# Sliding-window attention and two feed-forward layers: weight tiles without a place of their own use two buffers in turn

## The chip, the core and the metric

The kernel runs on one core of a Trainium2 chip, as one launch. The metric is the device time of one execution in microseconds (us). The engines are PE (TensorE: matmuls; PEld is its weight load), DVE (VectorE), ACT (ScalarE), POOL (GpSimd) and SP (SyncE, which here only issues DMAs). Each engine runs its own instructions in the order in which the program gives them, and waits on semaphores for the others.

## The reference

```python
S, D = 768, 64                      # 2 batches, 8 heads
scores = q @ k.T / sqrt(D) + bias   # 8 global keys, and the 96 newest keys of each query
a = softmax(where(keep, scores, -1e9))
x = (a @ v), heads joined           # 1536 tokens x 512
h = x @ w_in;  g = max(h, 0) + alpha * min(h, 0);      x = g @ w_out      # d_ff = 2048
h = x @ w_in2; g = (a0+a1 h+a2 h^2+a3 h^3) / (1+|b0||h|+|b1|h^2+1e-6);  out = g @ w_out2
```

All of it is float32. The four weight matrices arrive as float64 words, two 32-bit words for each number.

## The kernel before

**Split numbers.** Matmuls run on a rounded float32 format (fp32r). Each operand is kept as a high part and a low part, and a product is three passes: high by high, high by low, low by high.

**Weight jobs.** A weight matrix is cut into chunks `fc` of 128 hidden features, and a job prepares the "in" or the "out" half of one chunk, 128 x 512 numbers. `plan_weights` gives each job the tick at which it starts, and their order makes their number `n`. A job takes three ticks. At its start tick ACT scales the high words into `de` (L324). At the next tick DVE joins the words into `dx` with three instructions (L313, L314, L315); after them the code calls `load_more`, which has SP load the words of a later job (L269). At the third tick (L291 to L307) ACT, or POOL in the first slots, writes the high part `hi` (L301 or L303), and DVE writes the low part `lo` one tick later (L304).

**Where a job's tiles go.** Most jobs write into a slot of weight tiles. While attention runs only four such slots exist. The eight jobs of chunks 8 to 11, numbers 15 and 17 to 23, have no slot (`slot is None`): they write `hi` into `part1` and `lo` into `part2`, and both are sent to DRAM by `spill()` (L209 to L212). `spill()` is called at the third tick of the next job, just before that job's `hi`, and once more ahead of slot 15. SP issues these DMAs in the program's order, so they stand behind the L269 that was issued one tick earlier. The spilled chunks are read back (L217) when attention is over. `part0` to `part3` are tiles of the whole kernel, and `part3` holds the identity for transposes until then.

**Joint slots.** The stretch of the trace that matters here is that of the joint slots s = 8 to 15 (`joint_slot`, L848), in which a step of attention (two pairs of heads, step number u = 10 + s) runs beside one step of the first feed-forward layer. One slot gives each engine, in this order:

- PE: scores of step u (L431), values of step u-2 (L514, L516), `first(s)` = x @ w_in, 12 matmuls (L738), transposes of step u-1 (L490, L492), transposes of new keys or queries (L399, up to slot 10), `second(s-1)` = g @ w_out, 12 matmuls (L804);
- DVE: reciprocal (L465), the bias of step u with its row minimum (L446), `xlo` (L527), the low part of the job before (L304), the join of the next job (L313 to L315), the activation of `first(s)` (L744, L745);
- ACT: four exponentials (L453) with `xhi` among them (L526), copies `pt` (L501), `ghi` (L746), then the job's `hi` (L301) and the scaling of the next job (L324). In slot 8 four copies of results (L820) stand between `ghi` and `hi`;
- POOL: `glo` of the slot before (L747), L464, then the four normalisations of step u-1 (L470).

From slot 16 on attention is gone, its memory becomes the weight slots 4 to 15 (pool `late`, whose tiles each wait for what lay there), and PE runs one matmul after the other.

Of the kernel before, what the change touches and what calls it, by code (L numbers as in the profile page):

```python
# [8 lines left out]
F32 = mybir.dt.float32  # L9
F32R = mybir.dt.float32r  # L10
# [7 lines left out]
P = 128  # L18
# [4 lines left out]
DM = 512  # L23
# [29 lines left out]
def flat(t):  # L53
    return t.rearrange("p c f -> p (c f)")


def words(t):
    return flat(t).bitcast(F32)


class Kernel:
# [222 lines left out]
    def tick(self, on_act, start, spread=False):  # L284
        nc = self.nc
        if self.later:
            self.later.popleft()()
        while self.splits:
            self.splits.popleft()()
        self.join_step(5)  # L290
        if self.pipe and self.pipe[0][0] == "joined":  # L291
            _, n = self.pipe.popleft()
            m, fc, kind, slot = self.plan[n]
            self.spill()
            x = words(self.dx[n % 3])
            if slot is None:
                hi, lo = (t.bitcast(F32R) for t in self.part[1:3])
            else:
                hi, lo = (flat(self.slots[slot][kind, part]) for part in PARTS)
            if on_act:  # L300
                nc.scalar.copy(hi, x)  # L301
            else:
                nc.gpsimd.tensor_scalar(hi, x, 1.0, 1.0, ALU.mult, ALU.mult)  # L303
            self.splits.append(lambda: nc.vector.tensor_sub(lo, x, hi.bitcast(F32)))  # L304
            if m == 0 and fc < KEPT:
                for part, of in zip(PARTS, (hi, lo)):
                    self.unspilled.append((words(self.spilled[fc][kind, part]), of.bitcast(F32)))  # L307
        if self.pipe:
            _, n = self.pipe[0]
            self.pipe[0] = "joined", n  # L310
            low, e, y = self.staged(n)[:, :, :, 0], self.de[n % 2].bitcast(I32), self.dx[n % 3]
            self.join += [
                lambda: nc.vector.tensor_scalar(y, e, 3, None, ALU.logical_shift_left),  # L313
                lambda: nc.vector.scalar_tensor_tensor(y, e, -(2**31), y, ALU.bitwise_and, ALU.bitwise_or),  # L314
                lambda: nc.vector.scalar_tensor_tensor(y, low, 29, y, ALU.logical_shift_right, ALU.bitwise_or),  # L315
                self.load_more,
            ]
        if not spread:
            self.join_step(5)
        if start:  # L320
            n = self.started
            self.started += 1
            self.pipe.append(("scaled", n))
            nc.scalar.mul(self.de[n % 2], self.staged(n)[:, :, :, 1].bitcast(F32), 2.0**-112)  # L324
# [37 lines left out]
    def attention_window(self, pool, moe):  # L362
# [10 lines left out]
        rec = [pool.tile([P, 4], F32, name=f"rec{i}") for i in range(2)]  # L373
        pt = [pool.tile([P, 2, 2, P], F32, name=f"pt{i}") for i in range(4)]
        self.first_saved = [pool.tile([P, DM], F32, name=f"first{d}") for d in range(NC)]

        def load(nm, i):
            if 2 <= i < NBLK:
                self.load_tokens(nm, i, raw[nm][i % 2])
# [258 lines left out]
    def attention_any(self, pool, moe):  # L638
# [16 lines left out]
        pt = pool.tile([P, NB, P], F32, name="a_pt")  # L655
        st = pool.tile([P, 4], F32, name="a_st")
        self.first_saved = [pool.tile([P, DM], F32, name=f"a_first{d}") for d in range(NC)]

        def transposed(dst, scale, nm, i):
            self.load_tokens(nm, i, ra)  # L660
            t = banks[7].rearrange("p (c t) -> p c t", c=NC)
            for c in range(NC):
                nc.tensor.transpose(t[:, c], ra[:, 2 * c : 2 * c + 2].rearrange("p h d -> p (h d)"), ident)
            nc.scalar.mul(dst, t, scale)
# [313 lines left out]
```

## Time and profile before

| | us |
|---|---|
| median of 3 runs | 677.8 |
| lowest and highest | 676.52, 678.18 |
| profiled execution | 678.08 |
| its span, first to last instruction | 676.2 |

| engine | busy us | share of the span |
|---|---|---|
| PE | 631.6 | 93% |
| DVE | 541.6 | 80% |
| ACT | 374.7 | 55% |
| POOL | 195.2 | 29% |

The profile is one execution with every instruction's start and length. Besides busy times it gives what each idle time of an engine ended on, and the chain of waits: from the last instruction back to what released it, and so on. Times below are from the span's start. 1.9 us of the profiled execution lie outside its span. The granted clock (PEclk) is the share of TensorE's full clock that it was allowed, 1.00 for 2.4 GHz.

### The profile page before, as it was taken

The page shows a single profiled execution, that of the slowest core. Times are in us where ns is not written, and L with a number is a line of the kernel's source. Part 1 is how long each engine was busy: PE and PEld are TensorE (multiplying, and loading weights), DVE is VectorE, ACT ScalarE, POOL GpSimd, SP SyncE. Part 2 cuts the span into 40 slices and gives each one's busy share as a digit, 9 for nine tenths or more (in the row PEclk, how much of TensorE's full clock was granted, in tenths as well). Part 3 has the DMA queues.
Part 4 walks back from the last instruction along what each step waited for, and adds up shares of the span by engine and source line. Part 5 has one row for each costly group of instructions (what it writes and reads, how often), then busy time and mean ns, then how long its engine had stood idle before and what let it go on. Part 6 is the DMA issues. An engine that isn't in the chain of part 4 may idle for free.

```text
span 676.2 us, 9567 instructions
## 1 busy us (share of the span) xinstructions
PE 631.6 (93%) x3250; PEld 510.2 (75%) x3250; DVE 541.6 (80%) x982; ACT 374.7 (55%) x782; POOL 195.2 (29%) x278
## 2 busy tenths in 40 slices
PE   7767998998988999999999998999999999999994
PEld 6656766776866888888888876888878888888782
DVE  3687789984654998876879999999999877786984
ACT  2775565665552432333324367777777766766662
POOL 4554334333232322222222212222222222222221
PEclk9897999998999999999999999999999999999997
DMA  8969488876667882331342231121110000300302
GB/s 164 198 165 271 136 249 251 258 221 222 186 225 235 291 317 89 99 121 31 126 155 63 70 117 31 32 95 39 55 62 1 1 1 1 124 1 0 126 0 69
DMA packets 84860, 82.83 MB, mean 123 GB/s; under 512 B 45312, under 2 KB 61952, under 8 KB 84800
## 3 DMA queue, kind: packets, MB, share of 16 engines
q1 hardware_dynamic: 84800, 82.11, 40.5%
q8 instruction: 28, 0.46, 0.3%
q14 instruction: 32, 0.26, 0.1%
HBM read 60.21 MB, written 19.92 MB: 119 GB/s over the span
## 4 chain that ended last, share of the span: by engine, by line
PE 59%; DVE 23%; ACT 6%; DMA 4%; issue 3%; POOL 3%; SPq 0%; DVEq 0%; ACTq 0%; POOLq 0%
PE bank L804 29%; PE bank L738 28%; DVE dx L314 3%; DVE dx L315 3%; DVE dx L313 3%; ACT prob L453 2%; DMA dwouthi_f<-part 2%; DVE prob L446 1%; DVE act L745 1%; DVE act L744 1%; DMA dwinhi_f<-part 1%; DVE xlo L527 1%; DVE klo L407 1%; DVE act L782 1%; POOL glo L747 1%
## 5 line engine op out<-in xcount | busy, mean ns | idle before, releaser
L747 POOL TENSOR_TENSOR glo<-act,ghi 128x512 fp32r<-128x512 f32 x48 | 65.6, 1367 | 225.6 <-ACT ghi L746 202.6
L789 POOL TENSOR_TENSOR glo<-act,ghi 128x512 fp32r<-128x512 f32 (+1 forms) x49 | 65.7, 1340 | 202.1 <-ACT ghi L785 187.2
L746 ACT CAST ghi<-act 128x512 fp32r<-128x512 f32 x48 | 29.8, 621 | 107.6 <-DVE act L745 99.7
L738 PE MATMUL bank<-xhi,winhi_f 128*128 128x512 f32 x256 | 68.4, 389 | 0.0
L738 PE MATMUL bank<-xhi,winlo_f 128*128 128x512 f32 x256 | 68.4, 389 | 0.0
L738 PE MATMUL bank<-xlo,winhi_f 128*128 128x512 f32 x256 | 68.4, 389 | 0.0
L453 ACT ACTIVATE prob<-prob,stat 128x232 f32<-128x232 f32 (+1 forms) x96 | 44.6, 466 | 38.8 <-DVE stat L446 38.7
L738 PEld LDWEIGHTS bank<-xhi,winhi_f 128*128 128x128 f32 x256 | 48.0, 188 | 10.0
L738 PEld LDWEIGHTS bank<-xlo,winhi_f 128*128 128x128 f32 x256 | 48.0, 188 | 10.0
L738 PEld LDWEIGHTS bank<-xhi,winlo_f 128*128 128x128 f32 x256 | 48.0, 188 | 10.0
L315 DVE SCALAR_TENSOR_TENSOR dx<-stage,dx 128x512 int32<-128x512 int32 x64 | 53.5, 836 | 2.2
L314 DVE SCALAR_TENSOR_TENSOR dx<-de,dx 128x512 int32<-128x512 int32 x64 | 51.8, 809 | 2.2
L756 ACT ACTIVATE stage<-bank 128x512 f32<-128x512 f32 (+1 forms) x49 | 28.8, 588 | 37.5 <-PE bank L738 37.4
L765 DVE SCALAR_TENSOR_TENSOR stage<-stage,abs_b 128x512 f32<-128x512 f32 (+1 forms) x49 | 36.2, 739 | 16.3 <-ACT stage L757 16.3
L470 POOL TENSOR_SCALAR prob<-prob,rec 128x232 f32<-128x232 f32 (+1 forms) x96 | 43.0, 464 | 21.7 <-DVE rec L465 14.3
L785 ACT CAST ghi<-act 128x512 fp32r<-128x512 f32 (+1 forms) x49 | 30.1, 614 | 26.5 <-DVE act L782 26.4
L324 ACT ACTIVATE de<-stage 128x512 f32<-128x512 f32 x64 | 42.4, 667 | 2.3 <-DMA stage<-in_moe_w_out_dram 2.3
L804 PE MATMUL bank<-wouthi_f,ghi 128*128 128x512 f32 x144 | 41.3, 392 | 0.6 <-ACT ghi L785 0.6
L744 DVE TENSOR_SCALAR act<-bank,al 128x512 f32<-128x512 f32 x48 | 35.8, 745 | 7.4 <-PE bank L738 7.2
L804 PE MATMUL bank<-wouthi_f,glo 128*128 128x512 f32 x144 | 41.2, 391 | 0.1
L804 PE MATMUL bank<-woutlo_f,ghi 128*128 128x512 f32 x144 | 41.0, 389 | 0.0
L313 DVE TENSOR_SCALAR dx<-de 128x512 int32<-128x512 int32 x64 | 38.0, 594 | 3.5 <-ACT de L324 3.5
(206 smaller groups left out, 1483.5 us busy)
## 6 DMA issues: line engine op xcount, KB each, us to landing
stage<-in_moe_w_in_dram SPq DMA_DIRECT2D x32, 512.0 KB, 4.1
stage<-in_moe_w_out_dram SPq DMA_DIRECT2D x32, 512.0 KB, 4.0
part<-saved_f SPq DMA_DIRECT2D x16, 256.0 KB, 4.3
va<-in_v_dram SPq DMA_DIRECT2D x13, 256.0 KB, 5.0
saved_f<-part SPq DMA_DIRECT2D x12, 256.0 KB, 3.7
out_dram<-part SPq DMA_DIRECT2D x11, 256.0 KB, 2.1
rawk<-in_k_dram SPq DMA_DIRECT2D x10, 256.0 KB, 4.7
rawq<-in_q_dram SPq DMA_DIRECT2D x10, 256.0 KB, 4.6
```

The lines of the kernel that those rows point to most:

```text
L313: lambda: nc.vector.tensor_scalar(y, e, 3, None, ALU.logical_shift_left),
L314: lambda: nc.vector.scalar_tensor_tensor(y, e, -(2**31), y, ALU.bitwise_and, ALU.bitwise_or),
L315: lambda: nc.vector.scalar_tensor_tensor(y, low, 29, y, ALU.logical_shift_right, ALU.bitwise_or),
L324: nc.scalar.mul(self.de[n % 2], self.staged(n)[:, :, :, 1].bitcast(F32), 2.0**-112)
L453: nc.scalar.activation(p[:, j - e, :w], p[:, j - e, :w], AF.Exp, bias=st[:, j : j + 1], scale=-1.0, accum_out=st[:, 4 + j : 5 + j],)
L470: nc.gpsimd.tensor_scalar(p[:, j, :w], p[:, j, :w], r[:, e + j : e + j + 1], 1.0, ALU.mult, ALU.mult)
L738: nc.tensor.matmul(bk, w["in", a][:, c, :], x[:, c, :], start=e == 0, stop=e == len(seq) - 1)
L744: nc.vector.tensor_scalar(t, h, 0.0, self.al[:, fc : fc + 1], ALU.min, ALU.mult)
L747: nc.gpsimd.tensor_tensor(lo, t, hi.bitcast(F32), ALU.subtract)
L765: nc.vector.scalar_tensor_tensor(w, w, self.ab[:, 0:1], ab, ALU.add, ALU.mult)
L789: nc.gpsimd.tensor_tensor(lo, u, hi.bitcast(F32), ALU.subtract)
L804: nc.tensor.matmul(y[d], lhs, rhs, start=begin and e == 0, stop=last and e == 2)
```

## The change

A pair of tiles `spare0`, `spare1` (128 x 512 float32 each) is added to attention's pool, behind `first_saved`. A job without a slot writes to `part1` and `part2` when its number is even and to the new pair when it is odd. The same pair is added to the general attention, which this input does not take.

```diff
             if slot is None:
-                hi, lo = (t.bitcast(F32R) for t in self.part[1:3])
+                hi, lo = (t.bitcast(F32R) for t in (self.part[1:3], self.spare)[n % 2])
             else:
                 hi, lo = (flat(self.slots[slot][kind, part]) for part in PARTS)
...
         self.first_saved = [pool.tile([P, DM], F32, name=f"first{d}") for d in range(NC)]
+        self.spare = [pool.tile([P, DM], F32, name=f"spare{d}") for d in range(2)]
...
         self.first_saved = [pool.tile([P, DM], F32, name=f"a_first{d}") for d in range(NC)]
+        self.spare = [pool.tile([P, DM], F32, name=f"a_spare{d}") for d in range(2)]
```

By their numbers jobs 15, 17, 19, 21 and 23 go to the new pair, and 18, 20 and 22 stay in `part1`, `part2`.

No instruction moves on any engine; what changes is which tile some of them touch and which semaphores they wait for. On ACT, from the end of slot 8 (the last L820 copy) to the `hi` of slot 9, with the semaphores in brackets (DMAHW are those of SP's DMAs), the order before is:

```order
L820 COPY first3_272<-bank7_89 128x512 [waits PE_49]
L301 CAST part1_76<-dx0_96 128x512 [waits DMAHW2_49,Activation_49]
L324 ACTIVATE de1_95<-stage3_93 128x512 [waits DMAHW0_49]
L453 ACTIVATE prob2_256,stat1_261<-prob2_256,stat1_261 128x232 [waits DVE_49,Pool_49]
L453 ACTIVATE prob2_256,stat1_261<-prob2_256,stat1_261 128x232 [waits DVE_49]
L526 CAST xhi2_107<-bank2_84 128x2x128 [waits PE_49]
L453 ACTIVATE prob3_257,stat1_261<-prob3_257,stat1_261 128x232 [waits DVE_49] x2
L501 COPY pt0_265<-bank0_82 128x512 [waits PE_49]
L501 COPY pt1_266<-bank1_83 128x512 [waits PE_49]
L406 CAST khi_248<-bank2_84 128x4x128 [waits DVE_49,PE_49]
L746 CAST ghi1_102<-act1_100 128x512 [waits DVE_49,Pool_49]
L301 CAST part1_76<-dx1_97 128x512 [waits DMAHW5_49,Activation_49]
```

The same rows of the changed kernel:

```order
L822 COPY first3_272<-bank7_89 128x512 [waits PE_49]
L301 CAST part1_76<-dx0_96 128x512
L324 ACTIVATE de1_95<-stage3_93 128x512 [waits DMAHW0_49,Activation_49]
L454 ACTIVATE prob2_256,stat1_261<-prob2_256,stat1_261 128x232 [waits DVE_49,Pool_49]
L454 ACTIVATE prob2_256,stat1_261<-prob2_256,stat1_261 128x232 [waits DVE_49]
L527 CAST xhi2_107<-bank2_84 128x2x128 [waits PE_49]
L454 ACTIVATE prob3_257,stat1_261<-prob3_257,stat1_261 128x232 [waits DVE_49] x2
L502 COPY pt0_265<-bank0_82 128x512 [waits PE_49,Activation_49]
L502 COPY pt1_266<-bank1_83 128x512 [waits PE_49,Activation_49]
L407 CAST khi_248<-bank2_84 128x4x128 [waits DVE_49,PE_49]
L748 CAST ghi1_102<-act1_100 128x512 [waits DVE_49,Pool_49]
L301 CAST spare0_273<-dx1_97 128x512 [waits DMAHW2_49,Activation_49]
```

The `hi` of job 18 (second row) waits for no DMA any more, and that of job 19 (last row) waits for DMAHW2, the DMA that job 18 waited for before, in place of DMAHW5, which is one job later. L324 and the two `pt` copies now also wait for an earlier instruction of ACT itself.

On DVE, after attention (`winlo14` and `woutlo14` being low parts in weight slot 14 of the pool `late`), before:

```order
L304 TENSOR_TENSOR winlo14_f_2359<-dx1_97,winhi14_f_2358 128x512 [waits DMAHW1_49,Activation_49]
L313 TENSOR_SCALAR dx2_98<-de1_95 128x512 [waits Activation_49]
L314 SCALAR_TENSOR_TENSOR dx2_98<-de1_95,dx2_98 128x512 [waits DVE_49]
L315 SCALAR_TENSOR_TENSOR dx2_98<-stage1_91,dx2_98 128x512 [waits DMAHW1_49,DVE_49]
L744 TENSOR_SCALAR act1_100<-bank0_82,al_66 128x512 [waits PE_49,Pool_49]
L745 SCALAR_TENSOR_TENSOR act1_100<-bank0_82,act1_100 128x512 [waits DVE_49]
L304 TENSOR_TENSOR woutlo14_f_2361<-dx2_98,wouthi14_f_2360 128x512 [waits Activation_49]
```

and in the changed kernel:

```order
L304 TENSOR_TENSOR winlo14_f_2361<-dx1_97,winhi14_f_2360 128x512 [waits DMAHW6_49,DMAHW1_49,Activation_49]
L313 TENSOR_SCALAR dx2_98<-de1_95 128x512 [waits Activation_49]
L314 SCALAR_TENSOR_TENSOR dx2_98<-de1_95,dx2_98 128x512 [waits DVE_49]
L315 SCALAR_TENSOR_TENSOR dx2_98<-stage1_91,dx2_98 128x512 [waits DMAHW1_49,DVE_49]
L746 TENSOR_SCALAR act1_100<-bank0_82,al_66 128x512 [waits PE_49,Pool_49]
L747 SCALAR_TENSOR_TENSOR act1_100<-bank0_82,act1_100 128x512 [waits DVE_49]
L304 TENSOR_TENSOR woutlo14_f_2363<-dx2_98,wouthi14_f_2362 128x512 [waits DMAHW7_49,Activation_49]
```

The two low parts gained a wait each, for DMAHW6 and DMAHW7: the last spill, job 23's, reads the new pair, and `winlo14` and `woutlo14` now lie where that pair lay.

## Rows read from the trace of the kernel before

**Rows 1.** Busy time by stretch: joint slots 8 to 14 by PE's starts, slot 16 on.

```profile
core 0: us, PE busy (x) PEld busy (x) DVE busy (x) ACT busy (x) POOL busy (x), PEclk, DMA share, GB/s
141.72:150.78 9.06, 8.97 (x67) 7.30 (x66) 7.01 (x19) 5.45 (x15) 3.52 (x6) 1.00 0.64 180
150.78:164.75 13.97, 10.71 (x66) 8.43 (x66) 6.81 (x19) 7.96 (x20) 3.66 (x7) 0.88 0.52 173
164.75:173.65 8.90, 8.90 (x66) 7.30 (x65) 5.33 (x16) 4.79 (x14) 2.83 (x6) 1.00 0.77 253
173.65:182.11 8.46, 8.46 (x62) 6.86 (x61) 4.24 (x15) 4.92 (x14) 3.24 (x6) 1.00 0.73 249
182.11:191.90 9.79, 8.91 (x61) 6.75 (x60) 5.06 (x17) 4.58 (x14) 3.27 (x6) 1.00 0.64 215
191.90:202.61 10.71, 9.32 (x61) 6.94 (x60) 5.50 (x17) 4.83 (x15) 3.25 (x6) 1.00 0.61 198
202.61:213.00 10.39, 8.63 (x48) 5.96 (x48) 5.25 (x9) 3.54 (x7) 3.26 (x6) 1.00 0.51 162
219.60:366.65 147.05, 147.05 (x650) 121.78 (x649) 123.19 (x165) 51.54 (x89) 35.91 (x27) 1.00 0.43 143
```

**Rows 2.** Waits of ACT, 150 to 212 us: sum, times, longest.

```profile
ACT part L301 <- DMA dwouthi_f<-part: 10.0, 3, 3.5
ACT part L301 <- DMA dwinhi_f<-part: 8.9, 3, 3.0
```

**Rows 3.** Chain of waits, 157 to 178 us: start, length, what.

```profile
162.61 4.54 DMA dwinhi_f<-part
...
172.96 4.60 DMA dwouthi_f<-part
```

**Rows 4.** Timeline of ACT: start, length, instruction, idle before it.

```profile
142.18 0.62 ACT L746 CAST ghi<-act 128x512 fp32r<-128x512 f32 x1 [1.40 <-DVE act L745]
...
145.32 0.49 ACT L453 ACTIVATE prob<-prob,stat 128x232 f32<-128x232 f32 x1 [1.41 <-DVE stat L446]
...
150.95 0.62 ACT L746 CAST ghi<-act 128x512 fp32r<-128x512 f32 x1 [1.91 <-DVE act L745]
151.48 2.04 ACT L820 COPY first<-bank 128x512 f32<-128x512 f32 x4
156.94 0.62 ACT L301 CAST part<-dx 128x512 fp32r<-128x512 f32 x1 [3.41 <-DMA dwouthi_f<-part]
...
163.63 0.62 ACT L746 CAST ghi<-act 128x512 fp32r<-128x512 f32 x1 [1.93 <-DVE act L745]
...
205.46 0.62 ACT L746 CAST ghi<-act 128x512 fp32r<-128x512 f32 x1 [2.42 <-DVE act L745]
```

**Rows 5.** Timeline of DVE, the same columns.

```profile
133.12 1.50 DVE L313 TENSOR_SCALAR dx<-de 128x512 int32<-128x512 int32 x1
...
144.85 0.37 DVE L446 CUSTOM_DVE_ANT_0 prob<-bank,bm 128x232 f32<-128x232 f32 x1
...
147.61 0.42 DVE L313 TENSOR_SCALAR dx<-de 128x512 int32<-128x512 int32 x1
...
153.35 0.37 DVE L446 CUSTOM_DVE_ANT_0 prob<-bank,bm 128x232 f32<-128x232 f32 x1
...
243.38 0.68 DVE L304 TENSOR_TENSOR winlo_f<-dx,winhi_f 128x512 fp32r<-128x512 f32 x1
```

**Rows 6.** Timeline of PE, slot 9.

```profile
159.82 0.66 PE L399 MATMUL bank<-part,rawk 128*128 128x128 f32 x4 [3.26 <-DVE xlo L527]
```

**Rows 7.** Timeline of POOL.

```profile
132.80 1.55 POOL L747 TENSOR_TENSOR glo<-act,ghi 128x512 fp32r<-128x512 f32 x1 [4.86 <-ACT ghi L746]
...
145.03 1.77 POOL L470 TENSOR_SCALAR prob<-prob,rec 128x232 f32<-128x232 f32 x4 [0.31 <-PE bank L738]
...
164.33 1.28 POOL L747 TENSOR_TENSOR glo<-act,ghi 128x512 fp32r<-128x512 f32 x1 [9.04 <-ACT ghi L746]
```

**Rows 8.** Timeline of SP's DMA issues.

```profile
210.98 0.32 SPq L212 DMA_DIRECT2D dwoutlo_f<-part  x1
```

## The prediction

> **What bounds the kernel now.** I read first how busy PE is by stretch, in the order of the joint slots [rows 1], and look for slots in which it isn't. Slots 10 and 11 are filled with matmuls to the last tenth (8.90 of 8.90 us, 8.46 of 8.46), and so is everything from slot 16 to 366 us (147.05 of 147.05). Slots 9, 12, 13 and 14 are not: they take 13.97, 9.79, 10.71 and 10.39 us for the same matmuls, or fewer. So only a change that shortens these four can move what follows, and what it takes from them reaches a stretch in which PE alone sets the pace.
>
> Next I ask who waits in this stretch. ACT's waits name one cause, the `hi` of a job without a slot, which waits for the DMA that spills the `hi` before it: 10.0 + 8.9 = 18.9 us in six waits of 2.9 to 3.5 us [rows 2]. They are jobs 18 to 23, in slots 8 to 13. The chain of waits shows the loop they close. The spill that starts at 162.61 takes 4.54 us [rows 3], then ACT goes on (`hi`, scaling, exponentials), DVE follows (`xlo`, low part, join), after the join SP issues L269, behind which the next spill stands, and at 172.96 that spill starts: one round in 10.35 us. The DMA is issued at the moment at which its buffer is wanted again.
>
> The ACT waits sum to 18.9 us, but that is not the worth of the change, as slots 10 and 11 show: ACT waits about 3 us in each, and PE loses nothing there, since it was behind with its work. The worth has to be counted on PE.
>
> **The wait that goes.** With two pairs a job's `hi` waits for the spill of the job two before. That spill was issued about one slot earlier than the one waited for now, so at 4.5 to 4.6 us of flight [rows 3] in a slot of some 8.5 us it has landed some 4 us before it is wanted. Job 18 goes to a tile that no spill reads. Jobs 15 and 17 share the new pair; they share a pair now as well, and the wait list [rows 2] holds none of the earlier ones, because job 16 lies between them. So I take all six waits as gone, and ask what is late next, slot by slot.
>
> **Slot 9.** In slot 8 the last copy ends at 151.48 + 2.04 = 153.52 us, and `hi` could start then; it starts at 156.94 after 3.41 us of waiting [rows 4]. Everything ACT and DVE do in slot 9 stands behind it, so `ghi` moves from 163.63 to 160.22. PE, which waited 3.26 us for `xlo` before its transposes [rows 6], has them as soon as it comes to them: `xlo` moves by 3.41, more than PE waited. The slot then holds the same 66 matmuls as slot 10, which took 8.90 us [rows 1]. 13.97 − 8.90 = **5.07 us**. Of this only 3.4 is the gap itself; the rest, some 1.7 us, is the clock: the granted clock of slot 9 is 0.88, of the slots around it 1.00 [rows 1], and the slow part comes after the idle stretch. With no gap in front I take it as given back.
>
> **Slots 10 and 11** are full already: 0.
>
> **The pace of ACT and DVE from there.** Without the wait one round from `ghi` to `ghi` is: `ghi` to the first bias 153.35 − 150.95 = 2.40 us, bias to the first exponential 145.32 − 144.85 = 0.47, exponential to the next `ghi` 150.95 − 145.32 = 5.63 [rows 4, 5]; together 8.50. The trace has one round of this form that waits for no spill, slot 7 to slot 8: 150.95 − 142.18 = 8.77 [rows 4]. It is longer by a `glo` of 1.55 us on POOL, which overlapped a job's low part on DVE, where the others take 1.28 (the rows at 132.80 and 164.33 show both kinds) [rows 7]. I take 8.50 and keep 8.77 as the other end. From 160.22 four rounds give 194.22 for the `ghi` of slot 13 (now 205.46).
>
> **Slots 12 and 13.** PE's slot 12 would start at 182.11 − 5.07 = 177.04. Its `first` needs the activation of slot 11, done by 160.22 + 2 × 8.50 = 177.22, and PE has scores and values (1 to 2 us) to do before it: no wait. Both slots have the matmuls of slot 11, which took 8.46: 9.79 − 8.46 = **1.33** and 10.71 − 8.46 = **2.25**. PE reaches slot 14 at 202.61 − 8.65 = 193.96.
>
> **Slot 14** has no scores, and PE now stands closer to ACT than before: its last transposes wait for the last normalisations, which follow `ghi` and `glo` of slot 13. This slot ends 213.00 − 205.46 = 7.54 us after that `ghi` [rows 1, 4], so at 194.22 + 7.54 = 201.76, **11.24 us** earlier than 213.00; this figure includes the 8.65 of the slots before. Job 23's low part on DVE may now fall onto `glo` there and stretch it by 0.27 (1.55 − 1.28). That leaves 11.0. With rounds of 8.77 in place of 8.50 `ghi` of slot 13 stands at 195.30, the slot ends at 202.84, and 10.2 are left. The other end is 11.24, without the stretched `glo`.
>
> **After attention** PE works without a gap until 366.65, and the work of the other engines is tied to PE's and to ACT's place, not to a time. DMA is busy for 0.43 of that stretch [rows 1], and the reload of the weights hangs on the end of attention, which comes earlier as well. So the 11.0 us pass through.
>
> **What the change adds.** No instruction, no byte. Two low parts on DVE gain a wait for job 23's spill, which SP issues at 210.98 [rows 8] and which lands some 4.6 us later; the first of the two runs at 243.38 [rows 5]. Both move together, so the wait is over 27 us before it is reached. If it weren't, the joins and activations queued behind it on DVE, and PE behind them, would pay. The extra waits of ACT for itself name work finished long before; I take them at nothing. From above the nearest rows give 0.1 us for one: an exponential starts 0.47 us after the start of a bias of 0.37 us that it waits for [rows 4, 5]. They fall on L324 and the copies, and only slot 9's L324 stands on the path: 0 to 0.1 us in all.
>
> The sum: the profiled execution took 678.08 us, and less 11.0 that is 667.1. It stands 0.28 above the median of the runs, so for the median I take 677.8 − 11.0 = **666.8 us**.
>
> **Rivals.** *POOL and DVE collide (671).* The join's first instruction takes 0.42 us alone and 1.50 when it falls onto a POOL instruction (the rows at 147.61 and 133.12, the latter beside the `glo` at 132.80) [rows 5, 7]. With the wait gone DVE's low part and join follow POOL's normalisations closely: in slot 8 these end at 145.03 + 1.77 = 146.80 [rows 7], and the join starts at 147.61, 0.8 us later. Should POOL slip by that much in slots 10 to 13, each round grows by 1.08, and 11.0 − 4 × 1.08 = 6.7 us are left: 671.1. For it: the low part runs just ahead of the join and takes 0.68 us [rows 5], so it stands only 0.1 to 0.2 us behind the last normalisation. Against: slot 8 has this spacing, and didn't collide.
>
> The Trainium skill ("SBUF — State Buffer", section "Who interferes with whom") says why such overlaps are dear: VectorE and GpSimd share a pair of ports that one holds for a whole instruction while the other is blocked, and a VectorE instruction with two inputs in SBUF, as the low part is, counts among those that need it. By this rule the low part would collide too if POOL slipped by its 0.1 to 0.2 us; by the rows it is the spacing that decides, and slot 8 shows it kept.
>
> *The gain is given back (677.8).* DVE is busy for 123.19 of the 147.05 us after slot 16 [rows 1]. If the weights of chunks 12 to 15 came to it at fixed times, from DMAs, PE would come to wait for DVE there. Against: PE waits for nothing in that stretch, and each job is started by the program's own steps.
>
> *The new wait on DVE decides (680).* If job 23's spill landed later than `winlo14` needs it, each us beyond that holds DVE and then PE. The wait has 27 us; it costs something from there on, it eats the 11.0 from 38 us on, and 2 us more would give 680. Nothing in the trace holds SP or a DMA for as long.
>
> *The waits don't go.* Were jobs 18 to 23 all of one parity, the new pair would sit idle. They aren't: the order of the jobs alternates (the numbers stand with the change), and this case is left without a chance of its own.
>
> **How the numbers follow.** The forecast, all six waits gone and PE full to slot 14, has 0.75, at 666.8, within 665.8 (677.8 − 11.24, less the 0.8 by which the runs scatter) to 668.4 (less 10.2, and 0.8 more). The collision or another partial gain has 0.15, at 671.1, between 668.4 and 672; given back 0.06; the wait on DVE 0.04. For 8 in 10 the range goes from 665.5 to 671.2. A measurement here can tell about 0.3%, 2 us, from no change: faster 0.90, same 0.06, slower 0.04.
>
> **What would show it.** Right: ACT's list of waits has no DMA for a `hi` any more; the granted clock of slot 9 stays at 1.00; rounds of `ghi` at 8.5 to 8.9 us in slots 9 to 13 in place of 10.3 to 10.8; slot 14 ends near 202 and PE is full from there on. Wrong: a `hi` that waits for a spill of two jobs before; joins of 1.5 us in slots 10 to 13; a new gap of PE in slot 14 or after 366; or a stretch from slot 16 on that is longer than before.

## The result and the profile after

The changed kernel takes 667.06 us (median of three runs, 666.91 to 667.26), against 677.75 before: 10.7 us less, ratio 0.9845 with a 95% interval of 0.9826 to 0.9865. A fourth run, at a mean granted clock of 0.751 over its whole length, took 787.14 us and is left out. The profiled execution took 666.91 us, its span 665.1, 11.1 less than before. The forecast was 666.8, in a range from 665.5 to 671.2.

On the page of the changed kernel (busy us, share of the span and instructions of an engine; then the chain that ended last, by engine) PE's share has risen from 93% to 95%, and the chain has 1% of DMA in it in place of 4%:

```profile
span 665.1 us, 9585 instructions
...
PE 628.9 (95%) x3250; PEld 509.8 (77%) x3250; DVE 541.8 (81%) x982; ACT 375.4 (56%) x782; POOL 195.7 (29%) x278
...
PE 60%; DVE 25%; ACT 6%; POOL 3%; issue 3%; DMA 1%; DVEq 0%; ACTq 0%; SPq 0%; POOLq 0%
```

Busy time by stretch, joint slots 8 to 15 by PE's starts and then slot 16 on, as in [rows 1]:

```profile
core 0: us, PE busy (x) PEld busy (x) DVE busy (x) ACT busy (x) POOL busy (x), PEclk, DMA share, GB/s
141.37:150.42 9.05, 8.96 (x65) 7.29 (x65) 7.00 (x19) 5.45 (x15) 3.52 (x6) 1.00 0.62 179
150.42:159.32 8.90, 8.90 (x65) 7.30 (x65) 5.85 (x18) 7.25 (x19) 3.24 (x6) 1.00 0.66 234
159.32:168.37 9.05, 8.96 (x65) 7.29 (x64) 6.67 (x19) 5.66 (x16) 3.25 (x6) 1.00 1.00 290
168.37:176.84 8.47, 8.47 (x61) 6.86 (x61) 5.95 (x17) 5.04 (x15) 3.25 (x6) 1.00 0.75 250
176.84:185.32 8.48, 8.48 (x61) 6.86 (x61) 5.58 (x16) 5.02 (x14) 3.25 (x6) 1.00 0.67 248
185.32:193.78 8.46, 8.46 (x61) 6.86 (x61) 5.27 (x16) 5.00 (x14) 3.25 (x6) 1.00 0.72 247
193.78:202.15 8.37, 8.26 (x49) 6.06 (x48) 3.03 (x6) 3.11 (x6) 4.98 (x7) 1.00 0.88 278
202.15:208.75 6.60, 6.60 (x41) 5.48 (x41) 1.87 (x3) 1.32 (x3) 0.25 (x1) 1.00 0.99 362
208.75:355.80 147.05, 147.05 (x650) 121.82 (x649) 123.21 (x165) 51.55 (x89) 35.92 (x27) 1.00 0.43 137
```

Slots 9, 12, 13 and 14, which took 13.97, 9.79, 10.71 and 10.39 us, take 8.90, 8.48, 8.46 and 8.37. Slot 9 has a granted clock of 1.00 in place of 0.88, and the stretch from slot 16 on is 147.05 us of full PE in both kernels.

ACT's waits from 150 to 212 us (sum, times, longest; the three largest). The two DMA rows of [rows 2], 18.9 us, have no successor here:

```profile
ACT ghi L748 <- DVE act L747: 16.3, 7, 4.1
ACT prob L454 <- DVE stat L447: 4.7, 4, 1.2
ACT pt L502 <- PE bank L493: 4.1, 4, 3.1
```

The wait of `ghi` for the activation was there before as well (13.0 us in six; the seventh here, of 4.1, is slot 15's). The other two rows are new: 4.7 us for the bias and 4.1 for PE's transposes, at places where PE has work. DVE's own wait for `xhi`, and through it for the late `hi`, falls from 16.7 to 3.6 us from slot 8 to the start of slot 15, and in the same stretch PE's list of waits is empty. The timeline of ACT (start, length, instruction, idle before it) shows slot 9, to be read beside [rows 4]. The `hi` of job 18 (L301) follows the copies at once, where it stood 3.41 us idle before; that of job 19 goes to the new pair, with no idle time either:

```profile
150.60 0.62 ACT L748 CAST ghi<-act 128x512 fp32r<-128x512 f32 x1 [1.91 <-DVE act L747]
151.13 2.04 ACT L822 COPY first<-bank 128x512 f32<-128x512 f32 x4
153.03 0.65 ACT L301 CAST part<-dx 128x512 fp32r<-128x512 f32 x1
...
159.78 0.62 ACT L748 CAST ghi<-act 128x512 fp32r<-128x512 f32 x1 [1.93 <-DVE act L747]
160.30 0.61 ACT L301 CAST spare<-dx 128x512 fp32r<-128x512 f32 x1
```

**The ledger.** The span is 11.1 us shorter. Slot 9 gives 5.07, slot 12 1.31, slot 13 2.25, slot 14 2.02; slot 10 takes 0.15 back; slots 8, 11 and 15 are alike within 0.01. That is 10.5. Slot 8 started 0.35 earlier in this execution (141.37 against 141.72; in a second profile of the changed kernel it started at 141.64), and from slot 16 to the end it is 0.25 shorter; no row ties either to the change.

### The profile page after: what moved, and what is told of

Read it like the earlier page. It is cut to its first block, busy times and chain, and to the rows that moved or that the text cites. A ratio compares the mean times of both kernels' runs of the same rounds, so it can differ in the third digit from the quotient of the medians.

```text
span 665.1 us, 9585 instructions
## 1 busy us (share of the span) xinstructions
PE 628.9 (95%) x3250; PEld 509.8 (77%) x3250; DVE 541.8 (81%) x982; ACT 375.4 (56%) x782; POOL 195.7 (29%) x278
## 4 chain that ended last, share of the span: by engine, by line
PE 60%; DVE 25%; ACT 6%; POOL 3%; issue 3%; DMA 1%; DVEq 0%; ACTq 0%; SPq 0%; POOLq 0%
PE bank L806 29%; PE bank L740 28%; DVE dx L314 3%; DVE dx L315 3%; DVE dx L313 3%; ACT prob L454 2%; DVE act L747 2%; DVE act L746 2%; DVE prob L447 2%; POOL glo L749 1%; DVE xlo L528 1%; ACT ghi L748 1%; DVE klo L408 1%; DVE act L784 1%; DVE stage L783 1%
## 5 line engine op out<-in xcount | busy, mean ns | idle before, releaser
L471 POOL TENSOR_SCALAR prob<-prob,rec 128x232 f32<-128x232 f32 (+1 forms) x96 | 43.4, 469 | 22.0 <-DVE rec L466 15.1
L324 ACT ACTIVATE de<-stage 128x512 f32<-128x512 f32 x64 | 42.5, 669 | 1.9 <-DMA stage<-in_moe_w_out_dram 1.9
```

The source lines that it names most:

```text
L471: nc.gpsimd.tensor_scalar(p[:, j, :w], p[:, j, :w], r[:, e + j : e + j + 1], 1.0, ALU.mult, ALU.mult)
```

## The experiments

Each is timed beside the kernel before; e1 to e4 share a chip (before 677.28 us there), so do the changed kernel's second run, e5, e7 and e8 (677.48), and e8b, e9 and e6 (677.79).

**e1: the new pair alone, without turns.** All eight jobs write to the new pair.

```diff
-                hi, lo = (t.bitcast(F32R) for t in (self.part[1:3], self.spare)[n % 2])
+                hi, lo = (t.bitcast(F32R) for t in self.spare)
```

> All eight jobs without a slot write to the new pair, none to part1 and part2, so the buffers don't take turns. Theory (the gain comes from the turns, that is from a hi that waits for the spill of the job two before in place of the one before): ACT has its six waits for a spill again, 18.9 us in all, and the time is that of the kernel before, 677.8 us within 1.5. Rival (what counts is where the tiles lie, or that part1 and part2 are free): 667 to 672 us with the waits still there.

Measured: 677.88 us, ratio 1.0 (0.9988 to 1.0012). ACT's waits for spills are back:

```profile
ACT spare L301 <- DMA dwouthi_f<-spare: 9.7, 3, 3.4
ACT spare L301 <- DMA dwinhi_f<-spare: 8.9, 3, 3.1
```

Neither other tiles nor another layout of the pool bring anything; the turns do.

**e2: only the first wait is taken away.** Jobs 15 and 17 use the old pair, 18 to 23 the new one.

```diff
+                hi, lo = (t.bitcast(F32R) for t in (self.spare if n >= 18 else self.part[1:3]))
```

> Jobs 15 and 17 write to part1 and part2, jobs 18 to 23 all to the new pair: only the first of the six waits goes, that of job 18 in slot 8. Theory (after slot 9 the loop of hi, exponentials, join, L269, spill goes on with rounds of 10.3 to 10.8 us and sets the pace): slot 9 takes 8.9 us, ghi of slots 9 to 13 come 3.4 us earlier than before and no more, PE gives back some of its 5.07 us by waiting in slots 10 to 13, slot 14 ends 3.4 us earlier: 674.4 us. Rival (PE's slots add up by themselves, so the gap and the slow clock of slot 9 are worth 5.07): 672.7 us. Second rival (the first wait is what matters, the others are hidden): 667 us.

Measured: 673.92 us, ratio 0.9958 (0.9944 to 0.9972), 3.4 us less. Five waits are left, and the windows of slots 9 and 10 show that slot 9 is whole and slot 10, 8.90 before, is now the one that waits:

```profile
ACT spare L301 <- DMA dwinhi_f<-spare: 8.8, 3, 3.0
ACT spare L301 <- DMA dwouthi_f<-spare: 5.7, 2, 2.9
```

```profile
151.03:159.93 8.90, 8.90 (x65) 7.30 (x64) 5.85 (x18) 7.25 (x19) 3.23 (x6) 1.00 0.66 235
159.93:170.25 10.32, 9.19 (x67) 7.29 (x66) 6.10 (x18) 5.41 (x15) 3.22 (x6) 1.00 0.82 250
```

Slot 9 gives 5.07 and slot 10 takes back 1.42; counted from the first values of slot 8 to those of slot 15, PE takes 66.0 us in place of 70.3. Slots 10 and 11 lost nothing before only because PE was already late; the five waits left over pace the later slots as before.

**e3: all waits but the first.** Jobs 15, 17, 18, 20 and 22 use the old pair, so job 18 still waits for job 17's spill.

```diff
+                hi, lo = (t.bitcast(F32R) for t in (self.spare if n in (19, 21, 23) else self.part[1:3]))
```

> Jobs 15, 17, 18, 20 and 22 write to part1 and part2, jobs 19, 21 and 23 to the new pair: the wait of job 18 stays, the other five go. Theory: slot 9 keeps its 13.97 us and its clock of 0.88; slots 10 and 11 stay at 8.9 and 8.5; slots 12 and 13 fall to 8.5; ghi of slot 13 comes at about 163.63 + 34 = 197.6, PE is the later one and ends slot 14 near 206.6 in place of 213.0: 671.4 us. Rival (the first wait is what matters): 677 us.

Measured: 672.11 us, ratio 0.9927 (0.991 to 0.9944), 5.2 less. One wait is left on ACT and one on PE, and the window of slot 9 has the low clock again:

```profile
ACT part L301 <- DMA dwouthi_f<-part: 4.1, 1, 4.1
```

```profile
PE bank L400 <- DVE xlo L528: 3.9, 1, 3.9
```

```profile
150.42:164.75 14.33, 10.44 (x65) 8.37 (x65) 6.80 (x19) 8.17 (x21) 3.37 (x7) 0.88 0.50 159
```

The wait on ACT is 4.1 us, but slot 9 is 14.33 − 8.90 = 5.43 us longer. PE waits for 3.9 of that; the rest, 1.5 us, comes with the lower clock. Four kernels agree on this: 0.88 with the gap (before and e3), 1.00 without (after and e2). By the medians the two halves, 3.4 and 5.2, sum to 8.6 of the 10.7 of both. PE's slots don't show such a loss: from slot 8's values to slot 15's e2 takes 4.3 us less than before and e3 6.0 less (64.3), 10.3 together, where the change takes 10.5. So the two parts very nearly add up on PE; where the medians lose the other 2 us isn't shown, and the single runs of a kernel scatter by 1 to 3 us.

**e4: one pair, and the spill issued at once.** The kernel before, with the spill of a slotless job moved from the next job's third tick to the tick after its own, ahead of that tick's join and so of its L269.

```diff
             self.splits.popleft()()
+        if self.homeless:
+            self.homeless = False
+            self.spill()
         self.join_step(5)
...
             if slot is None:
+                self.homeless = True
```

> The kernel before, with its one pair, but the spill of a job without a slot is issued at the tick after its hi, behind its low part and ahead of the L269 of the next join, in place of two ticks after. SP then has no wait for a join in front of the spill of hi. Theory (the wait is made by the spill's place in SP's queue, not by having one pair): the spill of hi starts 2 to 3 us after SP's loads for the slot, about 6 us before the next hi wants the tile, flies 4.6 us, and ACT's waits for spills fall from 18.9 us to under 1 us: 667.1 us within 1.5. Rival (one pair is too few: the spill starts only once the low part is written, and each of five hi waits some 0.75 us more): 670 us. Second rival (the flight is what costs): above 675 us.

Measured: 665.25 us, ratio 0.9823 (0.9807 to 0.984), 12.0 us less: more than was expected (667.1 within 1.5), and by its ratio the better kernel of the two, though it ran on another chip and the intervals overlap a little. ACT has no wait for a spill. In SP's timeline of the kernel before, the spill of job 17's `hi`, which the first of the six waits is for, stands behind the stores of the four copied results (L821), and that of job 18's behind the L269 of the next load:

```profile
152.08 1.81 SPq L821 DMA_DIRECT2D saved_f<-first  x4
153.95 0.55 SPq L212 DMA_DIRECT2D dwouthi_f<-part  x1
...
162.23 0.33 SPq L269 DMA_DIRECT2D stage<-in_moe_w_out_dram  x1
162.61 0.43 SPq L212 DMA_DIRECT2D dwinhi_f<-part  x1
```

In e4 (L213 and L270 are its L212 and L269, L306 is its L301) both stand ahead of these:

```profile
146.38 0.34 SPq L213 DMA_DIRECT2D dwouthi_f<-part  x1
...
154.72 0.40 SPq L213 DMA_DIRECT2D dwinhi_f<-part  x1
...
159.38 0.33 SPq L270 DMA_DIRECT2D stage<-in_moe_w_out_dram  x1
```

```profile
154.04 0.65 ACT L306 CAST part<-dx 128x512 fp32r<-128x512 f32 x1
```

The spill of job 18's `hi` is issued 7.9 us sooner. Some 3 of these come from the `hi` itself, which no longer waits. The rest is the queue: before, the `hi` of job 18 was done at 157.56 (the row at 156.94 in [rows 4]) and its spill went out 5.05 us later; in e4 it was done at 154.69 and its spill went out 0.03 later. In the changed kernel this spill still stands 5.1 us behind its `hi` (153.68 to 158.75); there it has the time, since the next `hi` uses the other pair.

So the missing buffer was one of two ways to see the same fault: the transfer was ready to go and stood in a queue behind one that wasn't. From the first values of slot 8 to those of slot 15 PE takes 59.5 us in e4 (143.39 to 202.87) and 59.8 in the changed kernel (142.39 to 202.15), 70.3 before. So the joint slots give 10.8 us in e4 and 10.5 in the change; most of the 1.8 us between their medians lies elsewhere (e7 to e9).

**e5: the last low part later.** The changed kernel, with job 23's L304 put off to the second half of slot 14.

```diff
-            self.splits.append(lambda: nc.vector.tensor_sub(lo, x, hi.bitcast(F32)))
+            low = lambda: nc.vector.tensor_sub(lo, x, hi.bitcast(F32))
+            if n == 23:
+                self.later += [lambda: None, low]
+            else:
+                self.splits.append(low)
```

> The changed kernel, with the subtraction of the last slotless job (number 23) put off to the second half of slot 14. Theory: in slot 14 the four normalisations on GpSimd were slowed by that subtraction of VectorE (2.20 us instead of 1.77), so they go back to 1.77 and slot 14 ends some 7.5 us after the conversion of slot 13 instead of 7.97: PE enters slot 15 about 0.4 earlier, time 666.7 (666.3 to 667.1). Rival: the normalisations are slow there for another reason; they stay at 2.2 and the time stays at 667.2.

Measured: 666.64 us, ratio 0.9835 (0.9818 to 0.9852); the changed kernel on the same chip has 667.32, so 0.7 less, with ranges that touch (666.15 to 667.22, 667.13 to 668.12). The timelines of POOL and DVE in slot 14 decide. First the changed kernel, where the low part stands inside the four normalisations (L471):

```profile
196.77 2.20 POOL L471 TENSOR_SCALAR prob<-prob,rec 128x232 f32<-128x232 f32 x4 [0.31 <-DVE rec L466]
```

```profile
196.90 0.87 DVE L304 TENSOR_TENSOR spare<-dx,spare 128x512 fp32r<-128x512 f32 x1
```

and then e5 (L475 is its L471), where they don't meet:

```profile
197.10 1.77 POOL L475 TENSOR_SCALAR prob<-prob,rec 128x232 f32<-128x232 f32 x4 [0.31 <-DVE rec L470]
```

```profile
199.59 0.68 DVE L304 TENSOR_TENSOR spare<-dx,spare 128x512 fp32r<-128x512 f32 x1
```

The window of slot 14 in e5 has PE full, and is 0.46 shorter than the changed kernel's 8.37:

```profile
194.11:202.02 7.91, 7.91 (x49) 6.07 (x49) 2.84 (x6) 3.11 (x6) 4.55 (x7) 1.00 0.61 200
```

**e6: three pairs.** Jobs 20 and 23 use two of the tiles that the first steps save from, so that three pairs take turns.

```diff
+                pair = self.part[1:3] if n in (18, 21) else self.first_saved[2:4] if n in (20, 23) else self.spare
+                hi, lo = (t.bitcast(F32R) for t in pair)
```

> The change with three pairs in turn (jobs 15, 17, 19, 22 into the spare pair, 18 and 21 into the old one, 20 and 23 into two of the tiles that the first steps save from). Theory: with two pairs no wait for a spill is left, so a third brings nothing: 667.2 (666.5 to 667.8), joint slots as with two. Rival: part of the wait is hidden in the two-pair kernel behind other waits; then a third pair gives 665 or less.

Measured: 666.94 us (665.71 to 667.97), ratio 0.9832 (0.9809 to 0.9855). From slot 8's values to slot 15's it takes 59.5 us. A third pair brings nothing that can be told apart: two were enough.

**The second run of the changed kernel, e7 (both edits) and e8: where e4's extra 1.8 us lie.** SP issues the last output transfers at 657.09 us in the changed kernel and at 657.45 in e4, but the span of e4 ends sooner, at 663.7 against 665.1. In its trace SP has 462 instructions in place of 450; the twelve more are waits on semaphores. e7 is e4 with the two pairs. e8 was meant to lengthen SP's stream by twelve transfers.

> The changed kernel itself once more, beside the next three. Every theory: 667.2 us (666.5 to 667.6); its span ends about 5.8 us after the end of the last output transfer's issue (659.27 of 665.1 in the profile of the change).

> Two pairs in turn and the early spill together. Theory: the waits of ScalarE are one sum of some 19 us that either edit removes whole, so joint slots 8 to 15 start within 0.3 us of those of either edit alone, and nothing is added. The end of the run then tells what the 1.9 us between the two edits are. If they come with SP's instruction stream (the early spill has 462 SP instructions in the trace, the change 450; the joint slots are alike), the last stretch from the end of the last issue to the end of the span is 4.0 us and the time is 665.3. Rival: the 1.9 us are a matter of the second pair of tiles (another layout of SBUF); then the last stretch is 5.8 us and the time 667.2.

> The changed kernel with twelve transfers of 4 bytes more in SP's queue, behind the first output transfer of the step sixth from the end, where SP has nothing else to do. Theory: the last stretch after the last output transfer depends on where SP's instruction stream ends, not on when the spills are issued; with twelve more instructions it falls from 5.8 to about 4 us, time 665.3. Rival: the stretch has to do with the early spill itself; it stays at 5.8 us and the time is 667.2 or, with SP's twelve issues in the way of an output transfer, up to 668.

Measured: the changed kernel again 667.32 us (ratio 0.985, 0.9832 to 0.9869); e7 664.78 (0.9807, 0.9789 to 0.9826); e8 667.45. In e8 the twelve transfers aren't in the trace: their condition names a step that stores no output. So e8 tells nothing of SP's length; it is the changed kernel once more. e7 has SP's 462 instructions and the short end, with the layout of the second pair, so the layout isn't the reason; the two edits don't add up in the joint slots (59.4 us).

**e8b and e9: SP's stream made longer, in the changed kernel and in the kernel before.**

```diff
+                if steps[n] == (1, 1, NF - 1, NF - 1) and d == 0:
+                    for i in range(12):
+                        nc.sync.dma_start(out=self.pad[0:1, i : i + 1], in_=self.ca[0:1].rearrange("(o n) -> o n", o=1))
```

> The changed kernel with twelve transfers of 4 bytes more in SP's queue, issued behind the first output transfer of the last step but one that writes output, where SP otherwise waits some 33 us for VectorE. Theory: the two kernels with an early spill have 462 SP instructions in the trace instead of 450 and end about 1.8 us sooner behind the last output transfer, because the end of the run waits for instruction loads; so a change of SP's length by itself moves the end: the stretch from the end of the last issue to the end of the span falls from 5.8 to about 4 us, and the time is 665.3 (665.0 to 665.8). Rival: the short end belongs to the early spill; the stretch stays at 5.8 and the time at 667.2 to 667.5.

> The same twelve transfers in the kernel before. Theory: SP's length acts by itself: 675.6 us, some 1.8 less than before, with the waits of ScalarE as before (18 to 19 us). Rival: 677.5, nothing gained.

Measured: e8b 666.32 us (665.59 to 667.2), its median outside what was expected, e9 675.85 (ratio to before 0.9968, 0.9954 to 0.9982), with 9.4 + 8.9 us of spill waits on ACT as before. The page's packets of the instruction queue, and from the timeline the last issues of SP (start, length), first of the changed kernel (its span, 665.1, is shown above):

```profile
q14 instruction: 33, 0.26, 0.1%
```

```profile
657.09 2.18 SPq L828 DMA_DIRECT2D out_dram<-part  x2
```

then of e8b, with its span:

```profile
span 663.8 us, 9598 instructions
...
q14 instruction: 31, 0.25, 0.1%
```

```profile
658.18 1.70 SPq L829 DMA_DIRECT2D out_dram<-part  x2
```

From the end of the last issue to the end of the span it is 665.1 − 659.27 = 5.8 us in the changed kernel and 663.8 − 659.88 = 3.9 in e8b. In the same way it is 6.1 before, 5.9 to 6.1 in e1, e2, e3 and e6, and 4.0, 4.1 and 4.2 in e4, e7 and e9, each in one profiled execution. All profiles with 450 SP instructions have the long end and 32 or 33 packets in that queue, all with 462 or 463 the short end and 31. The two kinds of longer stream (twelve more waits in e4 and e7, twelve more transfers in e8b and e9) share, as far as the traces show, only the length. So SP's length moves the end, by some 1.9 us, and with it most of what sets e4 ahead. By its times e9 shows it too: its interval leaves out no gain. In e8b the median moved by 1.0 against the changed kernel's on another chip and by 0.6 against e6's on its own, less than the 1.9 of the profile, in runs that scatter by 1.6; so of the size in time e8b decides little. Why the length matters wasn't tested. That the end waits for a load of instructions fits the packets, and is no more than argued.

## Why the prediction was right

**All six waits go, as forecast.** No `hi` waits for a spill in the rows above; e1 shows that it takes the turns, and e6 that two pairs are enough. The time to spare differs from the forecast's 4 us: job 19's `hi` starts 6.7 us after the issue of the spill that it waits for (153.59 to 160.30), job 21's 10.0 (167.31 to 177.31), and the spills of the new pair take 2.9 to 4.5 us to land, so some 2 us are left at the tightest.

**Slot 9: 5.07 forecast, 5.07 measured.** The part that was taken on trust, 1.7 us of clock after the gap, came: 1.00 instead of 0.88, 8.90 us for the slot. By [rows 1] PE was idle there for 3.26 us and busy for 10.71 with what now takes 8.90, so 1.81 go with the clock. e3, which leaves just this wait, brings both back.

**Slots 10 and 11: 0 forecast.** Slot 11 took 8.47 as against 8.46; slot 10 took 9.05, 0.15 more than forecast, with PE idle for 0.09. PE is now near enough to its partners to feel them: the trace puts 0.28 us of idle time of its weight load, ahead of the slot's values, down to DVE's `klo` (L408).

**The pace of ACT.** Rounds of 8.50 were taken, with 8.77 as the other end. The `ghi` come at 159.78, 168.28, 176.79, 185.63 and 194.18: rounds of 8.50, 8.51, 8.84 and 8.55. The last was forecast for 194.22. The four rounds took 0.40 more than forecast, and the first `ghi` came 0.44 earlier than forecast, 0.35 of that from the earlier start of slot 8. Most of the 0.40 stands in one place, ahead of the `ghi` at 185.63, where the chain of waits of the changed kernel has ACT waiting for nothing that the profile shows:

```profile
185.31 0.32 issue
185.63 0.63 ACT ghi L748
```

The same 0.32 stands there in the second profile of the changed kernel. In e4, e6 and e7 this round takes 8.55. Its cause isn't shown.

**Slots 12 and 13: 1.33 and 2.25 forecast, 1.31 and 2.25 measured.**

**Slot 14 was mis-sized as well.** It was to end 7.54 us after slot 13's `ghi`, plus 0.27 if job 23's low part fell onto `glo`. It ended 202.15 − 194.18 = 7.97 after it. The direction was right, the partner wrong and the term too small. With no scores in slot 14 DVE has no bias to compute, so the low part runs right behind `xlo` and falls onto the normalisations, not onto `glo`, and costs 0.43: 2.20 us in place of 1.77. PE's transposes need these one after the other, as the chain of waits of the changed kernel shows (start, length, what):

```profile
196.77 1.34 POOL prob L471 x2
...
198.15 0.33 PE bank L491
...
198.59 0.33 PE bank L491
...
199.02 0.33 PE bank L491
```

In e5, without the meeting, the slot ends 202.02 − 194.51 = 7.51 after that `ghi`, the 7.54 of the forecast.

By the Trainium skill ("SBUF — State Buffer", section "Who interferes with whom") a VectorE instruction with two inputs in SBUF and a GpSimd instruction that reads SBUF contend for one port pair. The trace agrees in kind, 0.68 to 0.87 on the one side and 1.77 to 2.20 on the other.

**So the sum is right by some luck.** Counted from slot 8 on the change gave 10.5 us, 0.5 less than the 11.0 of the forecast. On the path that ends slot 14 the four rounds lost 0.40 and the step behind the last `ghi` 0.16 (7.97 against 7.54 + 0.27), and the first `ghi` gave back 0.09. The 0.35 at the start and the 0.25 at the end, which no row ties to the change, filled the place.

**The rival of collisions in every round** (671) rested on low part and join slipping onto the normalisations. They kept their spacing, as slot 8 did: from slot 9 to slot 13 each low part took 0.68 us and each join's first instruction 0.42, the lengths of instructions undisturbed. Slot 10:

```profile
164.33 0.68 DVE L304 TENSOR_TENSOR spare<-dx,spare 128x512 fp32r<-128x512 f32 x1
164.93 0.42 DVE L313 TENSOR_SCALAR dx<-de 128x512 int32<-128x512 int32 x1
```

**The gain isn't given back, and DVE's new wait costs nothing.** Slot 16 on is 147.05 of 147.05 in both. Job 23's last spill is issued earlier than before (210.98 in [rows 8]), and the low part of `winlo14`, the fifth low part after attention, runs without idle time 35 us behind it:

```profile
197.79 0.32 SPq L212 DMA_DIRECT2D dwoutlo_f<-spare  x1
```

```profile
232.53 0.68 DVE L304 TENSOR_TENSOR winlo_f<-dx,winhi_f 128x512 fp32r<-128x512 f32 x1
```

**What the prediction didn't see** is in its own rows: a spill that stands behind L269 in SP's queue. It named this as part of the loop and went on to count buffers. e4 takes 10.8 us out of the joint slots with no tile at all, where the second pair takes 10.5.

## What to carry to other kernels

When an engine waits for the DMA that empties its buffer, ask first when that DMA was issued and what stood ahead of it in its queue: issuing it as soon as its data is there can be worth as much as a second buffer, and costs no memory. Count a removed wait on the engine that bounds the kernel, slot by slot, with what the gap does to its clock; ACT's 18.9 us of waits were worth 10.5 on PE, and the first of them, 3.4 us, was worth 5.07 in its slot. Look also at a slot of the series that lacks some instructions of the others, as slot 14 lacks the bias: they may have kept two others apart.

## What the runs showed of the hardware that was not expected

- The end of the run, after the last output transfer was issued, takes 5.8 to 6.1 us or 3.9 to 4.2, depending on 12 or 13 more instructions in SP's stream (e4, e7, e8b, e9).
- A VectorE subtraction of two tiles inside four GpSimd normalisations of 128 x 232 costs these 0.43 us on top of 1.77, and costs itself 0.19 on top of 0.68; 7.97 against 7.51 us on PE's path (e5).
